# Six score visits a token tile instead of eight: regrouping the forward softmax blocks of a layer-interleaved attention kernel

## The chip, the cores and the metric

The kernel runs on one core of one Trainium2 chip, as one launch. The metric is the device time of that launch in microseconds (us), taken as the median of several runs. A core has a matrix engine (TensorE, PE in the profile, with its weight loads as PEld), a vector engine (VectorE, DVE), a scalar engine for functions such as exp (ScalarE, ACT), a general engine (GpSimd, POOL) and an engine that issues the DMAs (SyncE, SP). Each runs its own queue in the order in which the kernel was written; semaphores order them against each other.

## The reference, cut to what matters

Four layers, A B A B, over 2048 tokens of width 640, and their gradients. A is linear attention; B is softmax attention of 32 heads of 20 elements over a window of 256 keys. Only the forward pass of the two B layers is touched:

```python
def _B_ref(x, wqkv, wo):
    B, S, D = x.shape                      # 1, 2048, 640
    H = 32; Dh = D // H; W = 256
    qkv = ...                              # x @ wqkv, split in heads
    scores = jnp.einsum("bhqd,bhkd->bhqk", q, k) * (Dh ** -0.5)
    idx = jnp.arange(S)
    mask = (idx[:, None] - idx[None, :] >= 0) & (idx[:, None] - idx[None, :] < W)
    scores = jnp.where(mask[None, None], scores, -1e9)
    p = _softmax(scores, axis=-1)
    o = jnp.einsum("bhqk,bhkd->bhqd", p, v)
    return (...o...) @ wo

x = A_x
x = x + _A_ref(_layernorm(x), A_wqkv, A_wo)
x = x + _B_ref(_layernorm(x), B_wqkv, B_wo)
x = x + _A_ref(_layernorm(x), A_wqkv, A_wo)
x = x + _B_ref(_layernorm(x), B_wqkv, B_wo)
# returned: x and the gradients of x and of the four weights
```

## The kernel before

Tokens are cut into 16 tiles of 128 (`TT`), heads into 8 groups of 4 (`G`). A token tile attends to itself and to the two tiles before it, so it has `nb` key blocks: 1 in tile 0, 2 in tile 1, 3 from tile 2 on. Layers are counted 0 to 3; layers 1 and 3 are the B layers, called the first and the second here.

The forward pass (`forward`) is one list of pieces, each with a place in time counted in slots. `plan.sort` orders the pieces by place, `slots` collects those whose place has the same whole part, and `run(n)` issues slot n. A piece that was put in the list earlier comes first where places are equal, since the sort keeps their order. All engines but SP keep this order; nothing reorders it. The first B layer has slots from `B1` = 138 on, eight a tile, and the second from `B3` = 302 on.

In a slot of a B layer, the following runs for one tile and one head group (a visit):

- `f_scores` comes first: 4 heads times `nb` blocks, each a matmul of 32 rows (a head's elements, padded) by 128 keys, at four row positions of PE at once, into `sT`, a PSUM tile of four banks with one buffer (`st.pS`). Then one ACT instruction (L383) takes the exp of it all into `eT` (pool `st.fpe`, five buffers).
- The other pieces of that slot, by place.
- `f_masks`, on POOL: one `affine_select` for the diagonal block (L389) and, with three blocks, one for the oldest (L393).
- `b_pv` of the visit two slots earlier: twelve matmuls of probabilities by values (tile `ops`, PSUM pool `st.po`, one buffer for half a tile's heads). After four groups DVE takes the reciprocal (L228) and writes the output (`ob`, L229).

The other pieces are the layers around: `plan_front` finishes the A layer before (`flip_pq`, `num`, `flip_o`, `proj`) and makes the B layer's queries, keys and values (`scale`, `flip_h`, `qkv`) for tiles up to four ahead; `plan_rear` finishes the B layer for earlier tiles (`flip_o`, `proj`) and in the first B layer starts the A layer behind it (`plan_feat`: `flip_h`, `feat` for `pk` and `v`, `outer`). The second B layer has `query` in `plan_front` in its place. Their places relative to a tile's first slot are written out by hand:

```python
f2=[-27.5, -23.6, -21.5, -20.6, -19.5, -17.9, -16.5, -15.1, -13.5, -7.8, -6.9, -5.5, -4.7, -3.8, -2.9,   # first B layer, plan_front
    11, 12, 13, 14, 17.6, 22.4, 23.3, 24, 25.1, 26.4, 27.3],                                               # plan_rear
f3=[-35.7, -30, -26.5, -25, -24, -23.8, -22.5, -18, -16.4, -14, -12.1, -7.4, -6.8, -6, -4.9, -3.5, -1.7,  # second B layer, plan_front
    11.3, 12.4, 13.4],                                                                                     # plan_rear
```

Modulo eight these are the places in a tile's eight slots; -16.5, for instance, is the middle of slot 7, two or three tiles earlier. In order, `plan_front` of the first B layer has load, `flip_pq`, `num` twice, `flip_o`, `proj` twice, `scale`, `flip_h`, `qkv` six times; that of the second has `query` twice after the load. `plan_rear` has `flip_o`, `proj` twice, and in the first B layer `scale`, `flip_h`, `feat` four times, `outer` twice.

Steps that the prediction goes back to: `proj(1)` ends in the layer norm's `norm`, whose last instruction is a `pow` on POOL (L410), fed by the variance from DVE (L409). `feature` takes an exp on ACT (L557) and finishes on DVE (L558, L559), both reading the dense product in PSUM. A dense product (`dense`) is five matmuls of 320 columns. `flip` is five or six transposes on PE into PSUM, copied out by ACT (L163) or DVE (L165). All of these PSUM results share one pool of three tiles of one bank (`ps`, tag "m"): each waits until the result three before it has been read.

Of the kernel before, what the change touches and what calls it, by code (L numbers as in the profile page):

```python
# [10 lines left out]
ACT = mybir.ActivationFunctionType  # L11
ALU = mybir.AluOpType
AX = mybir.AxisListType
BF = mybir.dt.bfloat16
F32 = mybir.dt.float32
P = 128
D = 640
H = 32
DH = 20
HP = 32  # L20
T = 2048
TT = T // P
DT = D // P
G = H // 4
# [4 lines left out]
HS = (0, 6, 12, 18, 24, 26)  # L29
HB = 6  # L30
KB = HB * DH
# [21 lines left out]
class Kern:  # L53
# [157 lines left out]
    def b_pv(self, st, l, t, g, e, nb, rings, o):  # L211
        nc = self.nc
        q = g % 4
        if q == 0:
            st.ops = st.po.tile([P, HALF, HA], F32, name="ops")
            st.first = None
        for hh in range(4):
            for i in range(nb):
                ins = self.mm(st.ops[:, 4 * q + hh, :], e[:, hh, i * P:(i + 1) * P],
                              rings[i]["s"][:, 2, 4 * g + hh, 0:HA], st.first is None, i == nb - 1)  # L220
                if st.first is None:
                    st.first = ins
                else:
                    self.after(ins, st.first)
        if q == 3:
            c = g // 4
            r = self.r[l][:, t, c * HALF:(c + 1) * HALF]
            nc.vector.reciprocal(r, st.ops[:, :, DH])  # L228
            nc.vector.tensor_tensor(out=self.heads(o[:, c * CW:(c + 1) * CW]), in0=st.ops[:, :, 0:DH],  # L229
                                    in1=r.unsqueeze(2).to_broadcast([P, HALF, DH]), op=ALU.mult)  # L230
            if c == 1:
                self.dma(self.rows(self.o[l], t), o)


    def forward(self, st):
# [8 lines left out]
        nc = self.nc  # L244
        keep, early, lin = ExitStack(), ExitStack(), ExitStack()
# [1 line left out]
        st.sm = self.pool(keep, "fm", 4, side="right")  # L247
        st.fa = self.pool(keep, "fa", 3, side="right")
        st.xm = self.pool(keep, "xm", 5, side="right")
        st.fpe = self.pool(keep, "pe", 5, side="right")  # L250
        wo = self.pool(keep, "wo", 1, side="right")
        rings = {i: self.pool(keep if i in (0, 3, 4) else early, f"ring{i}", 1, side="right") for i in (0, 3, 4, 1, 2)}
        st.fb = self.pool(early, "fb", 3, side="right")
# [7 lines left out]
        pm = self.pool(first, "pm", 1, bass.MemoryType.PSUM, "right")  # L261
        st.M = [pm.tile([P, 512], F32, name=f"M{c}") for c in range(2)]
        st.ps = Two(ps, self.pool(first, "pf", 2, bass.MemoryType.PSUM, "right"))
        st.pend, st.behind, st.ring, st.va = [], 2, [], []
        X = {1: [{} for _ in range(TT)], 3: [{} for _ in range(TT)], 0: [{} for _ in range(TT)]}
        WA, WoB = vp.tile([P, DT, QT], BF, name="WA"), wo.tile([P, DT, D], BF, name="WoB")
        WB, WoA = wp.tile([P, DT, QT], BF, name="WB"), wp.tile([P, DT, D], BF, name="WoA")
# [6 lines left out]
        for i in range(3):  # L274
            v = vp.tile([P, H, HA], BF, name=f"va{i}")
# [8 lines left out]
        B1, B3, F = 138, 302, 6  # L284
        END = B3 + G * TT
        plan = []
# [10 lines left out]
        def scores():  # L297
# [3 lines left out]
            st.pS = self.pool(st.pSs, "pS", 1, bass.MemoryType.PSUM, "right")  # L301
        c1, c3 = 118, B1 + 144
        plan += [(c1, lambda: self.close_outer(self.mz[0], [m[0:KB, 0:3 * KA] for m in st.M])), (c1 + 9, lambda: self.turn_outer(st, self.mz[0], self.mzT[0])),
                 (B1, scores), (c3, lambda: self.close_outer(self.mz[2])),
                 (c3 + 9, lambda: self.turn_outer(st, self.mz[2], self.mzT[2]))]

        class B3_:
# [24 lines left out]
        def before(a):  # L332
            if a == 0:
                first_.update(enumerate(self.slots(self.plan_before(st, 3, 0, st.core, ((1, 2, 3, 8, 10), (2, 4, 5, 10, 12))), 16)))
            if first_[a] is not None:
                first_[a]()
        plan += [(END - 10 + a if a else END - 24, lambda a=a: before(a)) for a in range(13)]
        plan.sort(key=lambda x: x[0])
        slots = [[f for a, f in plan if int(a) == n] for n in range(int(plan[-1][0]) + 1)]

        def run(n):
            u, fs = None, slots[n]
            if B1 <= n < B1 + G * TT:
                if n == B1:
                    for f in fs:
                        f()
                    fs = []
                u = self.f_scores(st, *divmod(n - B1, G), X[1])
            elif B3 <= n < END:
                u = self.f_scores(st, *divmod(n - B3, G), X[3])  # L350
            for f in fs:
                f()
            if END - 12 <= n < END:
                self.warm(self.TAIL, st.ps.tile([P, 8, P], BF, name="warm", tag="m"))
            if u is not None:
                self.f_masks(*u)
                st.pend.append((l0(n), *u))
            if len(st.pend) > (st.behind if u is not None else 0):
                self.b_pv(st, *st.pend.pop(0))

        def l0(n):
            return 1 if n < B3 else 3
        for n in range(END):
            run(n)
        st.pSs.close()
        return [lambda n=n: run(n) for n in range(END, len(slots))], keep

    def f_scores(self, st, t, g, X):
        nc = self.nc
        if g == 0:  # L370
            X[t]["ob"] = st.fa.tile([P, D], BF, name="ob")
        nb = min(t, 2) + 1
        k0 = t - nb + 1
        rings = [st.ring[(k0 + i) % len(st.ring)] for i in range(nb)]
        qT = st.ring[t % len(st.ring)]["T"]
        s = st.pS.tile([P, 4, 512], F32, name="sT")
        for i in range(nb):
            for hh in range(4):
                r0 = HP * hh
                self.mm(s[:, hh, i * P:(i + 1) * P], rings[i]["T"][r0:r0 + HP, 1, g, :], qT[r0:r0 + HP, 0, g, :],  # L380
                        True, True, (r0, 0))
        e = st.fpe.tile([P, 4, 3 * P], BF, name="eT")
        nc.scalar.activation(e[:, :, 0:nb * P], s[:, :, 0:nb * P], ACT.Exp)  # L383
        return t, g, e, nb, rings, X[t]["ob"]

    def f_masks(self, t, g, e, nb, rings, o):
        nc = self.nc
        dg = e[:, :, (nb - 1) * P:nb * P]
        nc.gpsimd.affine_select(out=dg, in_=dg, compare_op=ALU.is_ge, fill=0.0, base=0,  # L389
                                pattern=[[0, 4], [1, P]], channel_multiplier=-1)  # L390
        if nb == 3:
            fr = e[:, :, 0:P]
            nc.gpsimd.affine_select(out=fr, in_=fr, compare_op=ALU.is_ge, fill=0.0, base=-1,  # L393
                                    pattern=[[0, 4], [-1, P]], channel_multiplier=1)

    def plan_ln(self, st, l, t, x, src, key, pool):

# [22 lines left out]
    def plan_front(self, st, la, lb, t, x, x_in, Wo, W, Wq=None):  # L420

        nc = self.nc
# [12 lines left out]
        def query(c):  # L435
            if c == 0:
                x["pqf"] = st.fb.tile([P, D], BF, name="pqf", bufs=2)
            self.feature(st, self.dense(st, x["h2T"], Wq, c * CW), x["pqf"][:, c * CW:(c + 1) * CW])()
            if c == 1:
                self.dma(self.rows(self.sv[la]["pqk"], t)[:, 0:D], x["pqf"])  # L440

        def flip_pq():
            x["pqT"] = self.flip(st.ps, st.fb, x["pqf"], "pqT", KB, 6, 0, nc.vector, [DH * h for h in HS])

        def num(c):
            if c == 0:
# [46 lines left out]
        if t == 0:  # L493

            b = -20
            a = [b - 10] + ([b - 4, b - 3] if Wq is not None else []) + [b, b + 1, b + 2, b + 4, b + 5, b + 6, b + 8, b + 10, *range(b + 12, b + 18)]
        else:
            a = list(PLACES["f2" if Wq is None else "f3"])
            if t <= 3:
                a[0] -= 6  # L500
        fs = [load] + ([lambda: query(0), lambda: query(1)] if Wq is not None else [])
        fs += [flip_pq, lambda: num(0), lambda: num(1), flip_o, lambda: proj(0), lambda: proj(1), scale, flip_h]
        fs += [lambda i=i: qkv(i // 2, i % 2) for i in range(6)]
        return list(zip(a, fs))
# [913 lines left out]
```

## Time and profile before

| What | us |
|---|---|
| Runs before (3): median | 2243.99 |
| lowest, highest | 2238.59, 2244.41 |
| Span of the profiled execution | 2242.3 |
| PE busy | 2071.8 (92%) |
| DVE busy | 1391.5 (62%) |
| ACT busy | 1350.6 (60%) |
| POOL busy | 1087.4 (48%) |
| ACT exp of the forward scores (L383), 256 instructions | 351.1 |
| POOL masks of the forward scores at L389 (256 instructions) | 162.9 |

The page gives the span of the profiled execution, from its first instruction to its last; the time of a run has what lies around it as well, so the profiled execution stands 1.7 us under the median of the runs. Busy times are of the whole program; the two stretches with forward B layers are about 115 to 390 us and 428 to 690 us from the start. In the profile's rows, a line such as L136 is that of a helper (every matmul), so rows are told apart by the tile names; `x12` counts merged instructions, and the brackets at the end give the idle time of that engine just before and what ended it. PE counts as busy while a matmul is in its pipeline, so a full PE need not be at its peak.

### The profile page before, as it was taken

The page shows a single profiled execution, that of the slowest core. Times are in us where ns is not written, and L with a number is a line of the kernel's source. Part 1 is how long each engine was busy: PE and PEld are TensorE (multiplying, and loading weights), DVE is VectorE, ACT ScalarE, POOL GpSimd, SP SyncE. Part 2 cuts the span into 40 slices and gives each one's busy share as a digit, 9 for nine tenths or more (in the row PEclk, how much of TensorE's full clock was granted, in tenths as well). Part 3 has the DMA queues.
Part 4 walks back from the last instruction along what each step waited for, and adds up shares of the span by engine and source line. Part 5 has one row for each costly group of instructions (what it writes and reads, how often), then busy time and mean ns, then how long its engine had stood idle before and what let it go on. Part 6 is the DMA issues. An engine that isn't in the chain of part 4 may idle for free. (4 is left out here: it accounts for less than half of the span.)

```text
span 2242.3 us, 76495 instructions
## 1 busy us (share of the span) xinstructions
PE 2071.8 (92%) x31941; PEld 1690.5 (75%) x31941; DVE 1391.5 (62%) x2858; ACT 1350.6 (60%) x2097; POOL 1087.4 (48%) x1887
## 2 busy tenths in 40 slices
PE   7889998899988999998879989999998899999999
PEld 5667776577767877777758868777777788888998
DVE  6778885877754778877747858788876233320000
ACT  5467787377776888877736768888876233330000
POOL 2046655156666577777643456777775312220000
PEclk9899999999998999999989999999999999999999
DMA  7498785698878588998899933999987999997753
GB/s 256 140 240 227 224 218 160 158 221 216 214 209 225 158 176 205 210 202 183 170 266 257 241 99 94 204 210 203 206 189 155 276 299 259 252 234 199 202 142 90
DMA packets 737484, 453.42 MB, mean 202 GB/s; under 512 B 477424, under 2 KB 713968, under 8 KB 736752
## 3 DMA queue, kind: packets, MB, share of 16 engines
q1 hardware_dynamic: 737136, 448.52, 79.8%
q8 instruction: 250, 4.10, 0.8%
q14 instruction: 98, 0.80, 0.1%
HBM read 213.09 MB, written 149.82 MB: 162 GB/s over the span
## 5 line engine op out<-in xcount | busy, mean ns | idle before, releaser
L663 DVE TENSOR_TENSOR ds<-dp,e 128x768 bf16<-128x768 f32 (+2 forms) x512 | 464.2, 907 | 176.0 <-PE s L136 62.4
L660 ACT ACTIVATE e<-s 128x768 bf16<-128x768 f32 (+2 forms) x512 | 395.7, 773 | 139.4 <-PE s L136 105.3
L383 ACT ACTIVATE eT<-sT 128x1536 bf16<-128x1536 f32 (+2 forms) x256 | 351.1, 1371 | 132.0 <-PE sT L136 130.1
L136 PE MATMUL wg<-rhs,lhs 128*128 128x240 bf16 (+1 forms) x3840 | 376.2, 256 | 11.7 <-DMA lhs<-o 9.2
L136 PEld LDWEIGHTS <-lhs 128*128 128x128 bf16 x3840 | 339.0, 98 | 26.6 <-DMA lhs<-o 10.7
L672 POOL TENSOR_SCALAR_AFFINE_SELECT e<-e 128x256 bf16<-128x256 bf16 x512 | 208.2, 408 | 248.9 <-ACT e L660 243.8
L136 PEld LDWEIGHTS <-dqT 128*128 128x128 bf16 x1920 | 171.3, 98 | 63.4 <-issue 10.4
L389 POOL TENSOR_SCALAR_AFFINE_SELECT eT<-eT 128x512 bf16<-128x512 bf16 x256 | 162.9, 637 | 108.1 <-ACT eT L383 106.5
L136 PE MATMUL acc<-slabqs,ds 128*128 128x20 bf16 x2880 | 210.4, 172 | 2.4 <-issue 1.0
L136 PE MATMUL dp<-slabvT,dT 32*128 32x384 bf16 (+2 forms) x1024 | 168.0, 320 | 43.8 <-DVE ds L663 39.3
L136 PE MATMUL acc<-ds,e 128*128 128x20 bf16 x2880 | 208.3, 171 | 0.0
L136 PEld LDWEIGHTS <-ds 128*128 128x128 bf16 x2880 | 188.1, 96 | 12.4 <-issue 4.1
L676 POOL TENSOR_SCALAR_AFFINE_SELECT e<-e 128x256 bf16<-128x256 bf16 x448 | 196.9, 439 | 0.0
L136 PEld LDWEIGHTS <-e 128*128 128x128 bf16 x2880 | 170.3, 96 | 11.2 <-issue 2.4
L1100 DVE CAST wr<-wg 128x240 bf16<-128x240 f32 (+1 forms) x72 | 27.3, 379 | 242.8 <-PE wg L136 236.6
L683 PE MATMUL flip<-ident,ds 128*128 128x128 bf16 x1944 | 169.8, 221 | 3.6 <-DVE ds L770 1.2
L136 PE MATMUL s<-slabkT,slabqT 32*128 32x384 bf16 (+2 forms) x1024 | 167.9, 323 | 4.2 <-ACT e L660 3.5
L1098 ACT CAST wr<-wg 128x240 bf16<-128x240 f32 (+1 forms) x48 | 16.2, 338 | 252.7 <-PE wg L136 234.8
L136 PE MATMUL dense<-WB,hnT 128*128 128x320 bf16 x960 | 164.5, 303 | 3.9 <-DVE o L457 2.4
L136 PE MATMUL dense<-WTA,dqT 128*128 128x320 bf16 x960 | 161.4, 299 | 2.2 <-DMA dqT<-dqa 1.9
L1016 POOL TENSOR_TENSOR dh<-dh,lg 128x640 f32<-128x640 f32 x32 | 46.0, 1438 | 239.3 <-DVE s L1013 239.3
L136 PE MATMUL acc<-slabks,dsT 128*128 128x20 bf16 x2880 | 147.3, 171 | 13.4 <-DMA dsT<-ds 12.9
(175 smaller groups left out, 4520.8 us busy)
## 6 DMA issues: line engine op xcount, KB each, us to landing
rhs<-dqkv SPq DMA_DIRECT2D x64, 480.0 KB, 5.1
s<-s SPq DMA_DIRECT2D x32, 768.0 KB, 3.8
T<-T SPq DMA_DIRECT2D x32, 768.0 KB, 4.0
dqkv<-dq SPq DMA_DIRECT2D x16, 960.0 KB, 5.5
dqkv<-dqa SPq DMA_DIRECT2D x32, 480.0 KB, 4.9
slabkT<-T SPq DMA_DIRECT2D x56, 256.0 KB, 4.6
slabvT<-T SPq DMA_DIRECT2D x56, 256.0 KB, 3.7
slabks<-s SPq DMA_DIRECT2D x56, 256.0 KB, 3.7
```

Of the source, the lines that this page charges most:

```text
L136: return self.nc.tensor.matmul(out, lhsT=lhsT, rhs=rhs, start=start, stop=stop, skip_group_check=True, **kw)
L383: nc.scalar.activation(e[:, :, 0:nb * P], s[:, :, 0:nb * P], ACT.Exp)
L389: nc.gpsimd.affine_select(out=dg, in_=dg, compare_op=ALU.is_ge, fill=0.0, base=0, pattern=[[0, 4], [1, P]], channel_multiplier=-1)
L660: nc.scalar.activation(u.e[:, :, 0:u.cw], s[:, :, 0:u.cw], ACT.Exp)
L663: nc.vector.tensor_tensor(out=d.ds[:, :, 0:d.cw], in0=d.dp[:, :, 0:d.cw], in1=d.e[:, :, 0:d.cw], op=ALU.mult)
L672: nc.gpsimd.affine_select(out=dg, in_=dg, compare_op=ALU.is_ge, fill=0.0, base=0, pattern=[[0, 2], [-1, P]], channel_multiplier=1)
L676: nc.gpsimd.affine_select(out=fr, in_=fr, compare_op=ALU.is_ge, fill=0.0, base=-1, pattern=[[0, 2], [1, P]], channel_multiplier=-1)
L683: nc.tensor.transpose(ps[:, 3 * j + i, :], f.ds[:, j, i * P:(i + 1) * P], self.ident)
L1016: nc.gpsimd.tensor_tensor(out=x["dh"], in0=x["dh"], in1=L["g"][:, i, :], op=ALU.add)
L1098: nc.scalar.copy(o[:, 0:w], ps[:, 0:w])
L1100: nc.vector.tensor_copy(o[:, 0:w], ps[:, 0:w])
```

## The change

The blocks of a tile, in the order of head group and key block, are taken four at a time, whatever group they belong to: 24 blocks in six visits from tile 2 on, 16 in four in tile 1, 8 in two in tile 0. Each visit has 16 score matmuls and one exp over 4 x 512 columns. The visits are pieces of the plan now, at the places `v * 8 / nv`; their masks stand 0.9 slots behind them, as many as before in all, and the value products of group g at g + 2.99, which is the end of the slot in which they were. The pool of `eT` has four buffers of 512 columns a head instead of five of 384, and `pqT` has two buffers instead of three. The places of all other pieces stay.

```diff
@@ b_pv
-                ins = self.mm(st.ops[:, 4 * q + hh, :], e[:, hh, i * P:(i + 1) * P],
+                ins = self.mm(st.ops[:, 4 * q + hh, :], e[i][:, hh, :],
@@ forward
-        st.fpe = self.pool(keep, "pe", 5, side="right")
+        st.fpe = self.pool(keep, "pe", 4, side="right")
...
-                 (B1, scores), (c3, lambda: self.close_outer(self.mz[2])),
+                 (B1 - 0.001, scores), (c3, lambda: self.close_outer(self.mz[2])),
...
+        for l, B in ((1, B1), (3, B3)):
+            for t in range(TT):
+                plan += [(B + G * t + a, f) for a, f in self.plan_scores(st, l, t, X[l])]
         plan.sort(key=lambda x: x[0])
         slots = [[f for a, f in plan if int(a) == n] for n in range(int(plan[-1][0]) + 1)]
 
         def run(n):
-            u, fs = None, slots[n]
...
-                u = self.f_scores(st, *divmod(n - B1, G), X[1])
-            elif B3 <= n < END:
-                u = self.f_scores(st, *divmod(n - B3, G), X[3])
-            for f in fs:
+            for f in slots[n]:
                 f()
             if END - 12 <= n < END:
                 self.warm(self.TAIL, st.ps.tile([P, 8, P], BF, name="warm", tag="m"))
-            if u is not None:
-                self.f_masks(*u)
-                st.pend.append((l0(n), *u))
-            if len(st.pend) > (st.behind if u is not None else 0):
-                self.b_pv(st, *st.pend.pop(0))
@@ f_scores and f_masks become plan_scores
+    def plan_scores(self, st, l, t, X):
+        nc = self.nc
         nb = min(t, 2) + 1
         k0 = t - nb + 1
+        blocks = [(g, i) for g in range(G) for i in range(nb)]
+        nv = len(blocks) // 4
+        home = {}
...
+        def visit(v):
...
+            s = st.pS.tile([P, 4, 512], F32, name="sT")
+            for j, (g, i) in enumerate(blocks[4 * v:4 * v + 4]):
+                for hh in range(4):
+                    r0 = HP * hh
+                    self.mm(s[:, hh, j * P:(j + 1) * P], ring(k0 + i)["T"][r0:r0 + HP, 1, g, :], qT[r0:r0 + HP, 0, g, :],
+                            True, True, (r0, 0))
+            e = st.fpe.tile([P, 4, 4 * P], BF, name="eT")
+            nc.scalar.activation(e, s, ACT.Exp)
+            for j, b in enumerate(blocks[4 * v:4 * v + 4]):
+                home[b] = e[:, :, j * P:(j + 1) * P]
+
+        def masks(v):
+            for g, i in blocks[4 * v:4 * v + 4]:
+                e = home[g, i]
+                if i == nb - 1:
+                    nc.gpsimd.affine_select(out=e, ...)      # diagonal, as before
+                elif nb == 3 and i == 0:
+                    nc.gpsimd.affine_select(out=e, ...)      # oldest block, as before
+
+        def values(g):
+            self.b_pv(st, l, t, g, [home[g, i] for i in range(nb)], nb, [ring(k0 + i) for i in range(nb)], X[t]["ob"])
+        plan = []
+        for v in range(nv):
+            at = v * G / nv
+            plan += [(at, lambda v=v: visit(v)), (at + 0.9, lambda v=v: masks(v))]
+        return plan + [(g + 2.99, lambda g=g: values(g)) for g in range(G)]
@@ plan_front
-            x["pqT"] = self.flip(st.ps, st.fb, x["pqf"], "pqT", KB, 6, 0, nc.vector, [DH * h for h in HS])
+            x["pqT"] = self.flip(st.ps, st.fb, x["pqf"], "pqT", KB, 6, 0, nc.vector, [DH * h for h in HS], bufs=2)
```

More of the change, by code (lines that the diff above doesn't have):

```diff
@@ L263, in forward @@
         st.ps = Two(ps, self.pool(first, "pf", 2, bass.MemoryType.PSUM, "right"))
-        st.pend, st.behind, st.ring, st.va = [], 2, [], []
+        st.ring, st.va = [], []
         X = {1: [{} for _ in range(TT)], 3: [{} for _ in range(TT)], 0: [{} for _ in range(TT)]}
@@ L341, in run @@
         def run(n):
-            u, fs = None, slots[n]
-            if B1 <= n < B1 + G * TT:
-                if n == B1:
-                    for f in fs:
-                        f()
-                    fs = []
-                u = self.f_scores(st, *divmod(n - B1, G), X[1])
-            elif B3 <= n < END:
-                u = self.f_scores(st, *divmod(n - B3, G), X[3])
-            for f in fs:
+            for f in slots[n]:
                 f()
@@ L354, in run @@
                 self.warm(self.TAIL, st.ps.tile([P, 8, P], BF, name="warm", tag="m"))
-            if u is not None:
-                self.f_masks(*u)
-                st.pend.append((l0(n), *u))
-            if len(st.pend) > (st.behind if u is not None else 0):
-                self.b_pv(st, *st.pend.pop(0))
-        def l0(n):
-            return 1 if n < B3 else 3
         for n in range(END):
@@ L366, in forward @@
         return [lambda n=n: run(n) for n in range(END, len(slots))], keep
-    def f_scores(self, st, t, g, X):
+    def plan_scores(self, st, l, t, X):
         nc = self.nc
-        if g == 0:
-            X[t]["ob"] = st.fa.tile([P, D], BF, name="ob")
         nb = min(t, 2) + 1
         k0 = t - nb + 1
[L374 to L394, printed above, removed]
+        blocks = [(g, i) for g in range(G) for i in range(nb)]
@@ new lines, in plan_scores, with ring @@
+        nv = len(blocks) // 4
+        home = {}
+        def ring(k):
+            return st.ring[k % len(st.ring)]
+        def visit(v):
+            if v == 0:
+                X[t]["ob"] = st.fa.tile([P, D], BF, name="ob")
+            qT = ring(t)["T"]
+            s = st.pS.tile([P, 4, 512], F32, name="sT")
[8 more added lines that the diff above has]
+                home[b] = e[:, :, j * P:(j + 1) * P]
@@ new lines, in masks @@
+        def masks(v):
+            for g, i in blocks[4 * v:4 * v + 4]:
+                e = home[g, i]
+                if i == nb - 1:
+                    nc.gpsimd.affine_select(out=e, in_=e, compare_op=ALU.is_ge, fill=0.0, base=0,
+                                            pattern=[[0, 4], [1, P]], channel_multiplier=-1)
+                elif nb == 3 and i == 0:
+                    nc.gpsimd.affine_select(out=e, in_=e, compare_op=ALU.is_ge, fill=0.0, base=-1,
+                                            pattern=[[0, 4], [-1, P]], channel_multiplier=1)
```

## The prediction

> **What bounds the kernel now.** The busy time by windows first. The forward pass of the first B layer (visits from 116 to 384 us) and of the second (428 to 689 us) are the only parts that the change touches.
>
> ```profile
> core 0: us, PE busy (x) PEld busy (x) DVE busy (x) ACT busy (x) POOL busy (x), PEclk, DMA share, GB/s
> 200.00:250.00 50.00, 49.96 (x864) 38.06 (x863) 42.85 (x114) 39.68 (x40) 30.30 (x51) 1.00 0.79 216
> 500.00:550.00 50.00, 47.09 (x863) 36.47 (x864) 37.24 (x97) 39.17 (x35) 30.82 (x52) 1.00 0.78 213
> ```
>
> TensorE (PE) is full in the first layer and has gaps in the second; ScalarE (ACT) is busy for 39 to 40 of 50 us. Next, the groups by shape give the price of a visit's exp, and the waits of four steady tiles (229.5 to 299.4 us, first layer) and of six (505.4 to 604.2 us, second) say who is late:
>
> ```profile
> L383 ACT ACTIVATE eT<-sT 128x1536 bf16<-128x1536 f32 x224 | 325.1, 1451 | 102.3 <-PE sT L136 101.2 <-POOL eT L393 0.5 <-POOL ds L786 0.5
> L383 ACT ACTIVATE eT<-sT 128x1024 bf16<-128x1024 f32 x16 | 16.4, 1025 | 13.5 <-PE sT L136 12.6 <-POOL eT L389 0.8
> L383 ACT ACTIVATE eT<-sT 128x512 bf16<-128x512 f32 x16 | 9.6, 598 | 16.2 <-PE sT L136 16.2
> ```
> ```profile
> POOL rs L410 <- DVE rs L409: 19.2, 8, 3.0
> ...
> PE sT L136 <- ACT eT L383: 4.3, 18, 0.3
> ```
>
> The first wait line is of the first layer: GpSimd (POOL) stands still up to 3.0 us at the `pow` of L410, because VectorE (DVE) is late with the variance. The second is of the second layer: PE waits for the exp, as `sT` has one buffer. Last the timeline, one steady tile of each layer. First layer:
>
> ```profile
> 246.96 1.45 ACT L383 ACTIVATE eT<-sT 128x1536 bf16<-128x1536 f32 x1 [0.25 <-PE sT L136]
> ...
> 247.02 0.49 DVE L559 SCALAR_TENSOR_TENSOR pqk<-dense,e 128x320 bf16<-128x320 f32 x1
> ...
> 248.58 0.45 PE L136 MATMUL ops<-s,eT 128*128 128x21 bf16 x12
> ...
> 248.95 0.55 POOL L410 TENSOR_TENSOR rs<-rs,mhalf 128x1 f32<-128x1 f32 x1 [3.00 <-DVE rs L409]
> ...
> 249.47 0.64 POOL L389 TENSOR_SCALAR_AFFINE_SELECT eT<-eT 128x512 bf16<-128x512 bf16 x1
> ...
> 250.89 0.45 PE L136 MATMUL ops<-s,eT 128*128 128x21 bf16 x12
> 251.09 0.71 ACT L163 COPY h2T<-flip 128x640 bf16<-128x640 bf16 x1
> 251.27 0.29 PE L136 MATMUL sT<-T,T 32*128 32x128 bf16 x8
> ...
> 251.75 1.45 ACT L383 ACTIVATE eT<-sT 128x1536 bf16<-128x1536 f32 x1
> ...
> 252.44 0.44 PE L160 MATMUL flip<-ident,hn 128*128 128x128 bf16 x5
> ```
>
> Second layer:
>
> ```profile
> 554.82 1.45 ACT L383 ACTIVATE eT<-sT 128x1536 bf16<-128x1536 f32 x1 [0.53 <-PE sT L136]
> ...
> 556.32 0.29 PE L136 MATMUL sT<-T,T 32*128 32x128 bf16 x8 [0.24 <-ACT eT L383]
> ...
> 564.83 1.45 ACT L383 ACTIVATE eT<-sT 128x1536 bf16<-128x1536 f32 x1 [0.58 <-PE sT L136]
> ...
> 566.66 0.41 DVE L558 TENSOR_SCALAR e<-e 128x320 bf16<-128x320 bf16 x1 [0.66 <-ACT e L557]
> ...
> 567.80 0.49 DVE L229 TENSOR_TENSOR ob<-ops,r 128x320 bf16<-128x320 f32 x1
> ...
> 568.44 0.45 PE L136 MATMUL ops<-s,eT 128*128 128x21 bf16 x12 [0.25 <-DVE ob L229]
> ```
>
> The exp rows that start at 246.96 and 264.41 are one tile apart: 17.45 us in the first layer. The second's is 16.45 (554.82 to 571.27). From visit to visit the timeline gives two limits. One is the loop over the single `sT`: sT to sT is never under 1.98 with a 1.45 us exp (554.34, 556.32, 558.30), so 0.53 lies around it. The other is PE's own work in the slot: a dense product of 5 matmuls 0.68 (249.24 to 249.93), a flip of 5 0.28, six flips 0.34, `num` or `outer` 0.17, the value products of a group 0.30, and a visit's twelve score matmuls with the change of tile shape 0.36 (0.28 from their start to the next product's, 0.08 before). The larger of the two gives each slot to within 0.2 us (0.46 at one). So the first layer is bound by PE's work, 17.03 + 0.42 of small waits, and the second by a mix.
>
> **Term 1, fewer and larger visits.** The three exp rows give 0.427 us per 512 columns, so 2048 columns take an estimated 1.45 + 0.43 = 1.88, and a column block costs the fixed 0.17 less often. Tile 0 has 2 visits, tile 1 has 4, the rest 6: 2 x (2 + 4 + 84) = 180 exps for 256, 338 us of ACT for 351. None of these 13 us is on the path by itself. PE loses two visits a tile, and each left gets four more matmuls (+0.07): 8 x 0.36 becomes 6 x 0.43, -0.30 a tile. The matmuls, the 480 masks (L389, L393) and every DMA stay as many as before. The loop becomes 1.88 + 0.53 + 0.06 = 2.47.
>
> **Term 2, uneven stretches.** The six visits, called V0 to V5 here, stand at 0, 1.33, 2.67, 4, 5.33 and 6.67 of a tile's eight slots; the pieces keep their places. PE's work from visit to visit, from the places and prices above (a piece with a visit's exact place comes ahead of it, having been put in the list earlier), comes to 3.11, 2.31, 3.02, 3.06, 2.10 and 3.08 in the first layer, together 16.7. The first, for instance: 0.34 from V0's start to its end, `qkv` 0.68, six flips 0.34, value products 0.30, two dense products 1.36, 0.09 for the next change of shape. Where a stretch is shorter than 2.47, PE waits: +0.16 and +0.37. That is 17.2 for 17.45.
>
> In the second layer it is 2.28, 2.38, 2.26, 2.08, 3.46 and 2.21; with the loop, 2.47 x 5 + 3.46 = 15.8 for 16.45.
>
> **Term 3, masks behind the pow (first layer).** V5 holds the last block of group 6 and all of group 7. Its masks are listed at 7.57, and POOL's `pow`, from `norm` in `proj(1)` (-16.5, so slot 7.5), ahead of them. Group 6's value products come at 8.99, in the next tile's slot 0. So far only group 7 sits behind that pow, and its products come one slot later: its second mask ends at 250.77, its products begin at 250.89. From V5 = 0: exp 0.53 to 2.40; the feature exp (L557) of `pk` is queued behind it and ends at 2.78; then DVE's min/add, 0.28 to the start of L559; from there to the pow 1.93 (247.02 to 248.95: `xm` and the statistics lie between) and to the end of the first mask 1.16 more (250.11): 6.15. PE is there at 3.08 (next V0) + 0.34 + 0.19 (`qkv(0)` waits for the PSUM tile that L559 reads; 0.12 today) + 0.68 + 0.34 = 4.6. It waits 1.55. Behind it on PE stand the two dense products of slot 1 and everything after; the masks of V0 behind the pow have time. Tiles 2 to 12 have both pieces: 11 times.
>
> The Trainium skill ("TensorE: Matmul & The Clock Gate", section "Architectural detail") says that the ACT and DVE queues are strictly first in, first out, as is GpSimd's, and that matmuls keep program order; this speaks against the change, and the 3.00 us of idle before the pow agree. By a queue that could pass the mask ahead, the term would be nought.
>
> **Term 4, the copy behind the exp (first layer).** `flip_h` of `plan_feat` (17.6, so 1.6) came ahead of slot 2's visit: its copy ran 251.09 to 251.80, ahead of the exp at 251.75. Now V1 (1.33) is listed before it. The copy starts when the longer exp ends, V1 + 2.35, and takes 0.70: 3.05. The PSUM pool `ps` has three tiles; after this flip come `outer`, `qkv`, and the next `flip_h`, which needs its tile. PE is there at 0.34 + 0.28 + 0.30 + 0.17 + 0.68 = 1.77. It waits 1.30 in tiles 2 to 13, 12 times; the loop's 0.16 of Term 2 lies inside that.
>
> First layer, steady: 16.7 + 0.19 + 1.55 + 1.30 + 0.37 = 20.1 for 17.45, 11 x 2.65 = +29; tile 13 about +1 (copy only). Tiles 0 and 1 lose six and four visits' changes of shape, 0.17 each: -1.7; tiles 14, 15 -0.6. Sum +28.
>
> **Term 5, DVE in the second layer.** Four dense products now lie between V4 and V5. `query(1)`'s feature exp waits for the 1.88 us exp; DVE needs 2.16 from the exp's end to the products of group 4 (566.28 to 568.44, shown). That is V4 + 4.56; PE is there at 3.46 + 0.34 = 3.80: wait 0.76 (0.46 today). DVE then still has `xm`, its statistics, `qkv(5)`'s copy and `pqT` to do in order: `num(0)`, now ahead of V0, waits an estimated 0.3 for `pqT`, and `qkv(1)` in slot 1 an estimated 0.6 for `num(0)`'s PSUM tile. The tile: 3.46 + (2.21 + 0.76 + 0.3) + (2.28 + 0.6) + 3 x 2.47 = 17.0 for 16.45, in ten tiles +5. Tiles 0, 1: -1.7; tiles 12 to 15, without front pieces and at the loop's floor, an estimated -0.4 each. Sum +2. Bounds: without these waits 10 x -0.6 - 3 = -9; with all of them twice as long, 1.66 a tile more, +19.
>
> **At nothing.** `pe` with 4 buffers: visit v+4's buffer was last read by value products two stretches earlier on PE, which keeps order; `pqT` with 2: it lives three slots of eight. If PE's order did not cover this, a visit's exp would wait for at most one stretch of value products, 0.30. Masks in the second layer stand before the pow (7.57 against 7.6), done 0.5 us or more before use. SP's queue keeps its order.
>
> **Sum.** The profiled execution has a span of 2242.3 us, the median of the runs is 2243.99, 1.7 more around it. +28 + 2 = +30: span 2272, time 2274. A measurement of this kernel tells some 0.3% (7 us) from no change.
>
> **Rivals.**
> - Faster: the waits of Terms 3 to 5 do not show, e.g. the copy gets in before V1's exp and the mask before the pow: 11 x -0.25, 10 x -0.6, edges -5: -14, 2230. Decides at mask end against V5 + 4.6. For it: PE's work and ACT's both shrink. Against: the listed order. 0.10.
> - Only one of Terms 3 and 4: +13 to +17, 2259. It needs another DVE or ACT order than today's rows. 0.15.
> - Group 6's products wait for all three masks of V5, if the wait is kept for the whole `eT` tile: 2 x 0.64 x 11 = +14, 2288. Nothing in the trace tells, since a visit had one group. 0.12.
> - PE's granted clock falls with the new gaps: windows 350 to 450 us show 0.93 at 41 to 42 of 50 us busy, and the first layer would have some 43. 16.7/0.93 is +1.3 x 11 = +14, 2288. Against: 600 to 650 us shows 1.00 at 44.03. 0.05. The Trainium skill ("TensorE: Matmul & The Clock Gate", section "A second HAM failure mode") has micro-idles between matmul groups throttle the clock; no run here shows it at gaps of 1.5 us.
> - The terms cancel within 7 us: 0.04.
>
> **Numbers.** Forecast 0.54, own range 2264 to 2284. With the neighbours on both sides 2250 to 2294, leaving out the faster case, the cancelling one and the far tails. Slower 0.86, same 0.04, faster 0.10.
>
> **Right or wrong.** Right: 180 exps of about 1.88; tiles of 20 us in the first layer and 17 in the second; PE `ops` waiting 1.5 us for POOL once a tile, and PE `flip` 1.3 us for ACT's copy. First-layer tiles of 17.2 would make Terms 3 and 4 wrong, second-layer tiles under 16 Term 5.

## The result, and the profile after

| | before | after |
|---|---|---|
| Median of 4 runs, us | 2241.51 | 2266.61 |
| lowest to highest | 2238.59 to 2244.41 | 2264.68 to 2269.53 |
| Span of the profiled execution | 2242.3 | 2267.7 |
| ACT busy | 1350.6 | 1342.2 |
| PE busy | 2071.8 | 2063.2 |

The changed kernel is slower: the ratio of the times is 1.0113, with a 95% interval of 1.0095 to 1.0131, or 25.1 us by the medians. ACT and PE both have less to do, as the change intends. The time is in the stretch that it touches. The view of the tile `eT` has a row of the value products with the start of their first and last matmul. Before, that row runs over 572.0 us; below it is the row after:

```profile
L136 PE MATMUL ops<-s,eT x2880: 172/172/227, 118.6 to 690.6; 128*128 128x21 bf16 x192
```
```profile
L136 PE MATMUL ops<-s,eT x2880: 172/172/227, 120.8 to 716.7; 128*128 128x21 bf16 x192
```

After, it is 595.9 us, 23.9 more, of the 25.4 that the spans differ by. The second layer's first exp starts 24.7 us later than before (453.0 for 428.2, by the timelines), of which 2.2 were there at the first value product; so the first layer cost 22.5 us and the second 1.4.

The groups by shape: one row takes the place of the three of before.

```profile
L376 ACT ACTIVATE eT<-sT 128x2048 bf16<-128x2048 f32 x180 | 337.9, 1878 | 131.2 <-PE sT L136 118.6 <-POOL eT L384 6.3 <-POOL prod L779 3.1
```

The busy time by windows, the same two as before:

```profile
core 0: us, PE busy (x) PEld busy (x) DVE busy (x) ACT busy (x) POOL busy (x), PEclk, DMA share, GB/s
200.00:250.00 50.00, 43.62 (x764) 32.14 (x762) 38.12 (x100) 35.55 (x31) 27.27 (x46) 1.00 0.70 196
500.00:550.00 50.00, 45.46 (x845) 34.34 (x842) 36.38 (x97) 37.79 (x28) 30.97 (x52) 1.00 0.93 213
```

PE, full in the first layer before (49.96), now stands still for 6.4 of 50 us, at a granted clock of 1.00. No engine took over as the bound: in the first layer all are less busy. So the engines wait for one another. The waits of four steady tiles of the first layer (219.7 to 297.9 us; total, times, longest):

```profile
POOL rs L412 <- DVE rs L411: 14.9, 4, 3.7
...
PE ops L136 <- POOL eT L384: 5.5, 4, 1.4
```

Once a tile PE stands 1.4 us at the value products until POOL has masked `eT`; POOL had itself stood 3.7 us at the `pow`, now L412, with that mask queued behind it. The timeline shows this in one tile, with V0 at 239.28 (V0 to V5 are the visits, as in the prediction):

```profile
239.28 0.29 PE L136 MATMUL sT<-T,T 32*128 32x128 bf16 x8
...
239.82 1.88 ACT L376 ACTIVATE eT<-sT 128x2048 bf16<-128x2048 f32 x1
...
241.18 0.55 POOL L412 TENSOR_TENSOR rs<-rs,mhalf 128x1 f32<-128x1 f32 x1 [3.73 <-DVE rs L411]
...
241.69 0.64 POOL L384 TENSOR_SCALAR_AFFINE_SELECT eT<-eT 128x512 bf16<-128x512 bf16 x1
...
242.38 0.41 PE L136 MATMUL ops<-s,eT 128*128 128x21 bf16 x10 [1.38 <-POOL eT L384]
...
244.10 0.23 PE L136 MATMUL sT<-T,T 32*128 32x128 bf16 x4
...
244.43 0.45 PE L160 MATMUL flip<-ident,hn 128*128 128x128 bf16 x5
...
244.63 1.88 ACT L376 ACTIVATE eT<-sT 128x2048 bf16<-128x2048 f32 x1 [0.68 <-PE sT L136]
...
245.02 0.36 PE L136 MATMUL outer<-va,pqk 128*120 128x126 bf16 x3
...
245.22 0.84 PE L136 MATMUL dense<-WB,hnT 128*128 128x320 bf16 x5
...
245.91 0.54 DVE L193 TENSOR_TENSOR macc<-outer,macc 120x378 f32<-120x378 f32 x1
...
246.37 0.48 DVE L488 CAST s<-dense 128x320 bf16<-128x320 f32 x1
...
246.41 0.69 ACT L163 COPY h2T<-flip 128x640 bf16<-128x640 bf16 x1
246.50 0.44 PE L160 MATMUL flip<-ident,hn 128*128 128x128 bf16 x5 [0.44 <-DVE macc L193]
...
247.15 0.23 PE L136 MATMUL sT<-T 32*128 32x128 bf16 x4
```

The three `sT` rows are the starts of V0, V1 and V2: 4.82 us, then 3.05. The mask at 241.69 is of group 6, whose last block came in the V5 before; it ends at 242.33, and PE goes on at 242.38. In the second stretch the copy `h2T` starts at 246.41, 1.78 after the start of the exp that it is queued behind. But the next `flip` starts at 246.50, during that copy, and also during DVE's `s`, which reads the dense product of 245.22. Of the three results before it only that of `outer` has been read by then: DVE's `macc` ends at 246.45, and that is what the flip waited for.

In the second layer, the waits of PE in six tiles (529.7 to 629.8 us):

```profile
PE ops L136 <- DVE ob L229: 4.2, 6, 0.7
PE dense L136 <- DVE o L459: 2.2, 6, 0.4
PE sT L136 <- ACT eT L376: 1.8, 6, 0.3
```

Each comes once a tile. The first of the three in the timeline:

```profile
573.73 1.88 ACT L376 ACTIVATE eT<-sT 128x2048 bf16<-128x2048 f32 x1 [0.58 <-PE sT L136]
...
575.97 0.44 DVE L560 TENSOR_SCALAR e<-e 128x320 bf16<-128x320 bf16 x1 [1.05 <-ACT e L559]
...
577.13 0.49 DVE L229 TENSOR_TENSOR ob<-ops,r 128x320 bf16<-128x320 f32 x1
...
577.77 0.45 PE L136 MATMUL ops<-s,eT 128*128 128x21 bf16 x12 [0.71 <-DVE ob L229]
```

From the exp's end (575.61) to the products of group 4 it is 2.16 us, by way of the feature exp, DVE's min and add, and `ob`.

The table has the steady tiles (tiles 3 to 12 in the first layer, tiles 2 to 11 in the second), from the start of a visit's first score matmul to the next visit's, in us:

| | V0→V1 | V1→V2 | V2→V3 | V3→V4 | V4→V5 | V5→V0 | tile | tile before |
|---|---|---|---|---|---|---|---|---|
| first layer, predicted | 4.85 | 3.61 | 3.02 | 3.06 | 2.47 | 3.08 | 20.1 | 17.45 |
| first layer, measured | 4.82 | 3.05 | 3.08 | 3.06 | 2.46 | 3.08 | 19.55 | 17.45 |
| second layer, predicted | 2.88 | 2.47 | 2.47 | 2.47 | 3.46 | 3.27 | 17.0 | 16.46 |
| second layer, measured | 2.78 | 2.46 | 2.46 | 2.46 | 3.46 | 3.05 | 16.68 | 16.46 |

### The profile page after: what moved, and what is told of

It reads as the page before. It is cut to its first block, busy times and chain, and to the rows that moved or that the text cites. A ratio compares the mean times of both kernels' runs of the same rounds, so it can differ in the third digit from the quotient of the medians.

```text
span 2267.7 us, 76356 instructions
## 1 busy us (share of the span) xinstructions
PE 2063.2 (91%) x31941; PEld 1673.8 (74%) x31941; DVE 1393.0 (61%) x2858; ACT 1342.2 (59%) x2021; POOL 1084.0 (48%) x1887
## 5 line engine op out<-in xcount | busy, mean ns | idle before, releaser
L376 ACT ACTIVATE eT<-sT 128x2048 bf16<-128x2048 f32 x180 | 337.9, 1878 | 131.2 <-PE sT L136 118.6
L384 POOL TENSOR_SCALAR_AFFINE_SELECT eT<-eT 128x512 bf16<-128x512 bf16 x256 | 163.5, 642 | 144.4 <-ACT eT L376 144.3
L387 POOL TENSOR_SCALAR_AFFINE_SELECT eT<-eT 128x512 bf16<-128x512 bf16 x224 | 143.3, 640 | 40.4 <-ACT eT L376 40.2
```

What stands on the lines that cost most here:

```text
L376: nc.scalar.activation(e, s, ACT.Exp)
L384: nc.gpsimd.affine_select(out=e, in_=e, compare_op=ALU.is_ge, fill=0.0, base=0, pattern=[[0, 4], [1, P]], channel_multiplier=-1)
L387: nc.gpsimd.affine_select(out=e, in_=e, compare_op=ALU.is_ge, fill=0.0, base=-1, pattern=[[0, 4], [-1, P]], channel_multiplier=1)
```

## The experiments

All of them are edits of the changed kernel, each timed against the kernel before on the same chip. The first four ran on one chip, the next four on another, the last on a third. The pieces of the other steps are moved by the lists of places `f2` (first B layer) and `f3` (second); the short diffs show the entries that change with their neighbours, and the names of the pieces.

**The masks ahead of the pow.** V5's masks go from 7.57 to 7.47, ahead of the `pow` at 7.5.

```diff
-            plan += [(at, lambda v=v: visit(v)), (at + 0.9, lambda v=v: masks(v))]
+            plan += [(at, lambda v=v: visit(v)), (at + 0.8, lambda v=v: masks(v))]
```

> The changed kernel with the masks listed 0.8 slots behind their visit instead of 0.9, so that those of V5 (now 7.47) stand ahead of the pow (7.5) of the first B layer; nothing else crosses. Theory (Term 3: group 6's value products wait on PE for V5's first mask, which waits behind the pow): the stretch V0 to V1 of the first layer falls from 4.82 to about 3.3 us, 11 times, and nothing else moves: 2266.6 - 17 = 2250. Rival: the DVE chain that makes the pow late is itself the limit, and the wait comes back at the next product that needs DVE (qkv, flip_h): V0 to V1 or V1 to V2 keeps over 1 us of it, less than 6 us gained, over 2260.

Measured: 2244.74 us (2240.6 to 2248.68), ratio 1.0022 (1.0009 to 1.0034). V0→V1 is 3.47 instead of 4.82, and the tile 18.20 instead of 19.55. PE's waits in five tiles (195.5 to 286.5 us) have no POOL row any more:

```profile
PE flip L160 <- DVE macc L193: 2.2, 5, 0.4
PE dense L136 <- DVE pqk L561: 1.5, 5, 0.3
PE sT L136 <- ACT eT L376: 1.5, 5, 0.3
```

The median fell by 21.9 us. The row of the value products of `eT` spans 581.2 us here, 14.7 fewer than the changed kernel's. Ten tiles at 1.35 and tile 13 at 3.25 would make 16.8, but the first two tiles of the layers took 2.6 us longer. The rest of the 21.9 is in parts that the edit doesn't touch (below). So a tenth of a slot in a list is worth some 15 of the 24 us that the stretch had lost. A wait of 0.3 for `qkv`'s PSUM tile (`pqk`) shows now, and the 0.4 at the flip stays; so V0→V1 is 3.47 and not the 3.3 that was expected.

**`outer` behind the flip.** Term 4 assumed that the three PSUM tiles of `ps` rotate strictly. Here the first `outer` goes behind the second flip, `num` stays.

```diff
-    f2=[... 25.1, 26.4, 27.3]    # outer(0)
+    f2=[... 25.1, 26.6, 27.3]
```

> The changed kernel with the first of the two outer pieces of the first B layer's rear moved from 2.4 to 2.6, behind qkv, flip_h and num of slot 2; all still ahead of V2. Theory (from the trace after: flip_h waits for the PSUM tile that outer's DVE accumulation reads): V1 to V2 falls from 3.05 to the loop's 2.46, -0.59 x 11 = -6.5, 2260. Rival (Term 4 as predicted: with strict rotation over three tiles, the third PSUM user behind the rear's flip waits for ACT's copy of it, which ends 3.05 behind V1): the third user is num now, V1 to V2 becomes about 3.5, +5, 2271.

Measured: 2264.91 us (2263.84 to 2268.05), ratio 1.0113 (1.0089 to 1.0137), as without the edit. V1→V2 is 3.31 (3.05 without the edit): neither the 2.46 of the theory nor the 3.5 of the rival. The timeline says why:

```profile
204.39 0.69 ACT L163 COPY h2T<-flip 128x640 bf16<-128x640 bf16 x1
204.43 0.31 PE L136 MATMUL num<-mz,pqT 120*128 120x126 bf16 x3 [0.30 <-DVE s L488]
...
205.13 0.33 PE L136 MATMUL outer<-va,pqk 128*120 128x126 bf16 x3 [0.39 <-ACT h2T L163]
```

`num` was given the tile of `qkv` (read by DVE's `s`), while the older tile, which the copy `h2T` still reads, went to `outer`. So here too the tiles did not come round in strict turn, and "each waits until the result three before it has been read", as the text on the kernel before has it, is not quite so. Two waits, 0.30 and 0.39, took the place of one of 0.44.

**The second query behind V5.** In the second layer, `query(1)` leaves the stretch of four dense products.

```diff
-    f3=[... -30, -26.5, -25, ...]    # query(1)
+    f3=[... -30, -25.9, -25, ...]
```

> The changed kernel with query(1) of the second B layer moved from 5.5 to 6.1, behind group 3's value products, so that DVE takes the reciprocal and output of groups 0 to 3 ahead of the query's feature step, which waits for ACT. Theory (Term 5: the order on DVE makes group 4's products late): V4 to V0 falls from 6.51 to about 6.1 and V0 to V1 from 2.78 to 2.46, -0.6 to -0.8 in ten tiles, 2259. Rival: the amount of DVE work between V4 and V0 sets it, not its order: no change, 2265 to 2268. First layer unchanged in both.

Measured: 2257.13 us (2251.82 to 2260.8), ratio 1.0074 (1.0047 to 1.0101). The tile is 16.10 instead of 16.68, V5→V0 2.46 instead of 3.05; V0→V1 stays 2.78. The row of the value products spans 592.6 us, only 3.3 fewer than without the edit: ten tiles save 5.7 us, but the passage from the first layer to the second took 2.5 us longer. The rest of the 9.5 us by the medians lies outside the stretch. PE's waits in six tiles (511.0 to 607.6 us):

```profile
PE dense L136 <- DVE o L459: 2.2, 6, 0.4
PE sT L136 <- ACT eT L376: 1.8, 6, 0.3
```

The wait for `ob` is gone. The one of `qkv(1)` for `num(0)`'s PSUM tile (the row with `o`) is as without the edit, so it doesn't hang on the query's place; that half of the expectation fell.

**Eight visits, listed by the plan.** This takes out the visits of four blocks and leaves the rest: the visits stand in the plan, `pqT` has two buffers, `eT` five of 384 columns a head.

```diff
-        nv = len(blocks) // 4
+        nv = G
...
-            for j, (g, i) in enumerate(blocks[4 * v:4 * v + 4]):
+            for j, (g, i) in enumerate(blocks[nb * v:nb * v + nb]):
...
-            plan += [(at, lambda v=v: visit(v)), (at + 0.9, lambda v=v: masks(v))]
+            plan += [(at - 0.001, lambda v=v: visit(v)), (at + 0.98, lambda v=v: masks(v))]
```

> The changed kernel's way of listing (visits, masks and value products as pieces of the plan, pqT with two buffers), but with eight visits a tile of one head group each, at the slots where they were before, and five eT buffers of 384 columns. Theory (the time lies in where six visits stand between the other pieces): as before, 2241.5 within 4 us, tiles of 17.45 and 16.46 us. Rival: the listing itself, or pqT's two buffers, costs part of the 25 us: over 2248.

Measured: 2236.34 us (2233.91 to 2244.89), ratio 0.9982 (0.9968 to 0.9995); tiles 17.45 and 16.46, those of before, and 573.1 us for the value products' row (572.0 before). The median is 1.2 us under the expected range; that of the kernel before was 2240.27 beside it. The listing and the second buffer cost nothing that shows.

**Both moves together.** The edits of the first and the third experiment.

> The changed kernel with both e1's masks at 0.8 and e3's query(1) at 6.1. Theory (two separate waits on PE, one a layer): the stretches are those of e1 in the first layer (18.2 a tile) and of e3 in the second (16.1), the gains add, 2266.6 - 11 x 1.35 - 3 - 10 x 0.59 = 2243 within 3. Rival (the layers share a limit, DMA or the clock): less than 15 us of it remains, over 2251.

Measured: 2246.03 us (2238.14 to 2250.28), ratio 1.0023 (1.0010 to 1.0037). The tiles are those of the two single edits, 18.20 and 16.10, and the stretch of the value products is 576.4 us for 595.9. Yet the median did not fall below that of the first experiment, though its stretch was 581.2. In the profiled executions the program behind the forward B layers, which no edit touches, took 1552 us here and 1547 there. So a few us of a median are not told apart here; the stretches are.

**The pieces spread over six stretches.** The masks ahead, and PE's pieces moved out of the long stretches into the short ones.

```diff
-    f2=[... 14, 17.6, 22.4, 23.3, 24, ...]    # plan_rear's flip_h; feat(1)
+    f2=[... 14, 21.3, 22.4, 22.6, 24, ...]
-    f3=[... -26.5, -25, -24, -23.8, ... -1.7, ...]    # query(1), flip_pq, num(0); qkv(5)
+    f3=[... -27.5, -25.4, -23.9, -23.8, ... -1.2, ...]
-            plan += [(at, lambda v=v: visit(v)), (at + 0.9, lambda v=v: masks(v))]
+            plan += [(at, lambda v=v: visit(v)), (at + 0.8, lambda v=v: masks(v))]
...
-                a = a[:5] + [x - 4 for x in a[5:]]
+                a = a[:4] + [x - 4 for x in a[4:]]
```

(The last tile's pieces from `flip_h` on stand four slots earlier.)

> The changed kernel with pieces moved so that no stretch between visits holds four dense products and at most one ACT copy stands ahead of an exp. First layer: masks at 0.8, rear flip_h 17.6 to 21.3 (V3 to V4), feat pk second half 23.3 to 22.6 (V4 to V5). Second: query(1) -26.5 to -27.5 (V3 to V4), flip_pq -25 to -25.4, num(0) -24 to -23.9, qkv(5) -1.7 to -1.2 (V5 to V0). Theory (time a tile is the sum over the six stretches of the larger of PE's work and the loop's 2.46): first layer 3.11 + 2.46 + 3.02 + 3.34 + 2.77 + 2.46 = 17.2, second 5 x 2.46 + 2.77 = 15.1; 2266.6 - 11 x 2.35 - 3 - 10 x 1.6 = 2222 within 6, below the kernel before. Rival (DVE at 12 to 15 us a tile is the next limit): waits for DVE come back, first layer over 17.8 or second over 16.0, over 2234.

Measured: 2227.15 us (2225.28 to 2227.59), ratio 0.9942 (0.9925 to 0.9958). The first layer's stretches are 3.12, 2.46, 3.01, 3.34, 2.78 and 2.46, a tile of 17.17; the second's 2.93, 2.46, 2.46, 2.77, 2.46 and 2.46, 15.55, not the 15.1 expected: V0→V1 kept a wait. The value products' row spans 557.2 us. The windows show PE full again in the first layer and fuller than before in the second (48.28 for 47.09):

```profile
200.00:250.00 50.00, 49.45 (x880) 36.70 (x878) 42.93 (x115) 40.61 (x36) 31.83 (x53) 1.00 0.80 231
500.00:550.00 50.00, 48.28 (x888) 36.85 (x888) 39.41 (x107) 40.44 (x29) 33.46 (x55) 1.00 0.93 223
```

The only wait that PE has left in six tiles of the first layer (192.5 to 295.5 us) is of 0.2:

```profile
PE num L136 <- DVE macc L193: 1.0, 6, 0.2
```

**Spread further.** From the kernel above, the first layer's `num(1)` and `outer(1)` also go a stretch earlier.

```diff
-    f2=[... -21.5, -20.6, -19.5, ... 26.4, 27.3]    # num(1); outer(1)
+    f2=[... -21.5, -21.4, -19.5, ... 26.4, 26.6]
```

> e6 with num(1) (-20.6 to -21.4) and the second outer (27.3 to 26.6) moved from V2-V3 into V1-V2 of the first layer, which has 0.4 us to spare for PE there. Theory (the larger of PE and loop): first layer 16.8 a tile, 4 us below e6. Rival (DVE order): V1 to V2 then holds 4.3 us of DVE work in 2.46, the PSUM tiles come free late, and the tile is as long as e6's or longer, 0 to +10 us.

Measured: 2234.2 us (2227.74 to 2239.78), ratio 0.9971 (0.9954 to 0.9988). V1→V2 grows from 2.46 to 3.30, V2→V3 falls from 3.01 to 2.77 only, and the tile is 17.76. PE has the same pieces to do; the order of the engines that feed it is not the same: `num` has a second wait now, 0.2 for ACT's copy `hnT`, beside that for `macc`.

**Eight visits with the query moved.** Is the gain of the spread that of the six visits, or would eight do as well? This tries it with one piece, in the second layer only.

```diff
-    f3=[... -30, -26.5, -25, ...]    # query(1), in the kernel with eight visits
+    f3=[... -30, -26.005, -25, ...]
```

> e4's eight visits with query(1) of the second layer behind group 3's value products in the same slot (-26.5 to -26.005). Theory (the same DVE order costs the eight-visit kernel its 2.44 us slot): that slot falls to about 2.03, -0.4 x 10 = -4 against e4, no more, since every slot is then at the loop's 1.98 or PE's 2.03. Rival: the wait for DVE moves into the next slots: no change.

Measured: 2236.66 us (2228.8 to 2240.69), ratio 0.9985 (0.9971 to 0.9999). The slot that had four dense products falls from 2.44 to 2.03 and the tile to 16.06. That is 0.2 from the loop over `sT`, 8 x 1.98 = 15.84. Six visits have theirs at 6 x 2.46 = 14.76. The value products' row spans 566.3 us, 6.8 fewer than with eight visits and the query in its old place, though the ratio is the same within its interval. A spread of the first layer's pieces was not run with eight visits.

**Spread, with `num` later in the second layer.** From the spread kernel.

```diff
-    f3=[... -23.9, -23.8, -22.5, ...]    # num(0), num(1), flip_o
+    f3=[... -23.3, -23.2, -21.4, ...]
-    f2=[... -2.9, 11, 12, ...]    # plan_rear's flip_o
+    f2=[... -2.9, 10.6, 12, ...]
```

> e6 with, in the second layer, num (-23.9, -23.8 to -23.3, -23.2) behind qkv(0) and flip_o from -22.5 to -21.4 behind query(0); in the first layer the rear's flip_o from 11 to 10.6, from V2-V3 into V1-V2. Theory: second layer, V0 to V1 falls from 2.93 to 2.46, because qkv(1) then takes a PSUM tile that DVE frees early instead of num's, -0.47 x 10 = -4.7; first layer, V1-V2 stays at 2.46 and V2-V3 falls from 3.01 to 2.73, -0.28 x 11 = -3; 2227 - 8 = 2219. Rival (DVE is the limit of the first layer's V1-V2, as e7 showed with 1.5 us more of DVE work there): V1-V2 grows by 0.3 or more and eats the first layer's gain; second layer as above, 2222 or more.

Measured: 2218.46 us (2211.79 to 2222.75) for 2240.54 of the kernel before, ratio 0.9901 (0.9886 to 0.9916). It beats both kernels, the one before and the changed one (1.0113). In the second layer V0→V1 falls from 2.93 to 2.54, V2→V3 rises from 2.46 to 2.56, and the tile is 15.26, but for two that took 15.4 and 15.9. In the first, V1→V2 and V2→V3 are 2.90 and 2.76 for 2.46 and 3.01: the earlier `flip_o` costs 0.2, and the tile is 17.35. The same row of `eT` as above now spans 553.5 us, 18.5 fewer than before the change and 3.7 fewer than that of the spread kernel; the 8.7 us between the medians of the two spread kernels, taken on different chips, are mostly outside it:

```profile
L136 PE MATMUL ops<-s,eT x2880: 171/172/227, 118.9 to 672.4; 128*128 128x21 bf16 x192
```

## Why the prediction was right, and where a size was off

**Term 1** holds: 180 exps of 1878 ns (1.88 predicted), 337.9 us (338), and a loop of 2.46 (2.47). ACT's busy time fell by 8.4 us while the time rose by 25.1.

**Term 2** holds. The stretches without a further wait came at 3.08, 3.06 and 3.08 in the first layer (3.02, 3.06, 3.08 predicted) and 3.46 in the second; the shorter ones stand at the loop. In the second layer the spread kernel shows what the uneven stretch cost: V4→V5 fell from 3.46 to 2.46, V3→V4 rose by 0.31 and V0→V1 by 0.15, which makes the tile 15.55 for 16.10. In the first layer the unevenness alone would have left a tile of 17.2 by the sum; the waits of Terms 3 and 4 came on top.

**Term 3** holds and is the main cause: 4.82 for 4.85 predicted, and moving that mask alone gave back 1.35 us a tile and 14.7 of the stretch's 23.9 us. The Trainium skill ("TensorE: Matmul & The Clock Gate", section "Architectural detail") has these queues strictly first in, first out; the trace agrees: POOL idled 3.73 us at the `pow`, up to 241.18, and the input of the mask behind it was ready from the end of V5's exp at 238.61. The rival by which group 6's products wait for all three masks of V5 is refuted: PE went on 0.05 us after the first of them.

**Term 4** has the right place and the wrong size. The copy did end where it was put, at V1 + 3.00 (3.05 predicted), but V1→V2 was 3.05, not 3.61. The step of it that failed is "after this flip come `outer`, `qkv`, and the next `flip_h`, which needs its tile". The tile that `flip_h` got was `outer`'s, and it waited 0.44 for DVE, which reaches `macc` late, behind `r` (245.21) and `ob` (245.50). The second experiment showed the same from the other side. The wait came in tiles 3 to 13; in tile 2, where it was predicted too, V1→V2 took 2.49. The 0.56 a tile is nearly all of the difference between 20.1 and 19.55, and over eleven tiles 6 us, about the gap between the +30 of the sum and the +25 measured. So the time, 7.4 us under the 2274 forecast, came out near the low end of the range: 4.9 by the sum and 2.5 because the median of the kernel before, with a fourth run, was 2241.51 and not 2243.99.

**Term 5**: group 4's products waited 0.71 (0.76 predicted; before, the wait itself was 0.25 by the row that the prediction shows, and 0.46 is what that slot took beyond the loop), and 2.16 from the exp's end is what was measured before too. `qkv(1)` waited 0.36 (0.6). The 0.3 of `num(0)` for `pqT` does not show. So the tile is 16.68 and not 17.0, and the layer +1.4 instead of +2.

**At nothing**: the eight-visit kernel shows the listing and `pqT`'s buffers free. `pe`'s four buffers were not tried by themselves; no wait for them shows.

**The other rivals.** The granted clock did not fall in the steady tiles: 1.00 from 150 to 350 us, with PE at 43.62 of 50 in the window shown. The Trainium skill's rule on micro-idles ("TensorE: Matmul & The Clock Gate", section "A second HAM failure mode") does not show at those waits of 1.38 us once a tile. In tile 13, where PE waits 1.72 us, the clock did fall right behind the wait: from 360.0 to 363.4 us it was 0.51, and five matmuls of a dense product took 1.54 us instead of 0.84. So the rival of the falling clock came about in one place, for 1.2 us and not 14. "Only one of Terms 3 and 4" lay nearest: by its size, Term 4 counted half, and the measured time lies halfway between that rival's 2259 and the forecast. Faster was possible, but only with the places of the masks and of other pieces changed.

**Tile 13 and the edges.** The prediction had eleven tiles at 20.1 and about +1 for tile 13. The trace shows ten, tiles 3 to 12, at 19.55 (+21.0 together), and tile 13 at 19.71 for 16.95 (+2.8). Its first stretch took 6.02 us: the mask of tile 12's V5 is late there too, and the half clock behind that wait adds 1.2. In the kernel with `outer` moved, the same stretch has a wait of 1.71 at a clock of 1.00 and took 4.82. Tile 2 is 0.2 longer than before, and tiles 0, 1, 14 and 15 up to the start of the second layer together 1.6 shorter.

**Left open.** Why the clock fell behind a wait of 1.72 us in the changed kernel, and in that with the second query moved, but not behind one of 1.71 in the kernel with `outer` moved, no run here shows.

## What to carry to other kernels

Where engines are fed from one list of places, a change in the number of visits moves every step against every other: write down, for each queue, what now stands ahead of what, and find the engine that idles at the head of a queue while work stands behind it. Here a saving of busy time became time only after the late mask was moved and the long stretches were shortened: six visits cost 1.1% with the old places and gained 1.0% with the new ones. How much of that 1.0% eight visits would gain with places of their own is not shown; one moved piece brought their tile in the second layer to 16.06, where six visits reached 15.26. Don't assume that a pool's tiles come round in turn; in these two kernels they did not where a release was late; ask the timeline which reader ended just before the tile's next writer.

## What the runs showed of the hardware

- An exp from PSUM grows linearly up to 2048 columns: 598, 1025, 1451 and 1878 ns, 427 for each 512. The Trainium skill ("ScalarE: Activation LUTs", section "What ACT_TABLE_LOAD costs") has 186 ns and 0.833 ns a column for an instruction with immediate scale and bias, by which 2048 would be an estimated 1892; the trace is within 1%.
- PE's waits of 1.38 us, one in each tile of 19.55, left its granted clock at 1.00. Behind the one wait of 1.72 us (tile 13 of the first layer) it was 0.51 for 3.4 us; behind the same wait in the kernel with the second query moved it was 0.53, and in that with `outer` moved (1.71 us) 1.00.
- Parts of the program that no edit touches varied between profiled executions: from the start of the last value product to the end of the span it was between 1542.9 and 1552.2 us, and the first visit started anywhere from 113.5 to 117.7 us. Of the first 30 us, the kernel before had 18.29 us of PE busy at a granted clock of 1.00, and the changed one 15.37 at 0.98, though the change leaves that part as it was.
